# Early row maxima of an attention stage, placed in the Fourier stage by running counts of engine time instead of a fixed list of positions

## The chip, the core and the metric

The kernel runs on one NeuronCore of a Trainium2 chip. The engines of that core work side by side: the matmul engine (PE, with PEld for its weight loads), the vector engine (DVE), the activation engine (ACT), the general engine (POOL) and the engine that issues most transfers (SP). Each takes its own instructions in program order, and they wait for each other through semaphores. The metric is the device time of one execution in microseconds; lower is better. Three executions of the kernel before took 3697.72, 3699.8 and 3702.65 us, so its median is 3699.8 us.

## What is computed

Two identical layers run one after the other on a sequence of 2048 rows of 512 values. Each layer is a Fourier stage and an attention stage, both on a layer-normed input and both added to the input:

```python
def _A_ref(x, dft_seq_re, dft_seq_im, dft_hid_re, dft_hid_im):
    a = jnp.einsum("bsd,ed->bse", x, dft_hid_re)
    b = jnp.einsum("bsd,ed->bse", x, dft_hid_im)
    return jnp.einsum("ts,bse->bte", dft_seq_re, a) - jnp.einsum("ts,bse->bte", dft_seq_im, b)

def _B_ref(x, wq, wk, wv, wo):        # 32 query heads of 16 values, one key head, one value head
    ...
    scores = jnp.einsum("bhqd,bkd->bhqk", q, k) * (Dh ** -0.5)
    p = _softmax(scores, axis=-1)
    o = jnp.einsum("bhqk,bkd->bhqd", p, v)
    return o.transpose(0, 2, 1, 3).reshape(B, S, H * Dh) @ wo

x = x + _A_ref(_layernorm(x), ...)    # Fourier stage, layer 0
x = x + _B_ref(_layernorm(x), ...)    # attention stage, layer 0
x = x + _A_ref(_layernorm(x), ...)    # layer 1, the same two again
x = x + _B_ref(_layernorm(x), ...)
```

The softmax needs the largest score of every row of every head: 32 heads times 2048 rows, each over 2048 keys.

## The kernel before, in words

**Precision.** Values are split into a high and a low part, and a product is three matmuls (high by high, high by low, low by high; `mm3`, lines 85 to 88).

**Fourier stage** (`phase_a`, line 562). The output rows are made in four blocks (`tb`) of 512 rows. A block has 32 steps `n` in which the transforming matrix is multiplied with the normed input (the result is called z, held in the four PSUM banks named x), 16 for the real part (c=0) and 16 for the imaginary part (c=1). Then come the z-by-hidden-matrix products of that block (`y_rows`, line 415, also in the x banks). From step 16 on, a product with 128 rows of the array is written as two products with 64 rows that run beside each other (`z_rows`, line 676); after each first phase ACT copies a few values to `junk` (line 693), which orders the two halves. At the end of c=0 and of c=1, `evac` (line 665) moves z from the x banks to SBUF with ACT, DVE and POOL.

**Work that rides along.** While block tb+1 is in its first steps, the tasks of `prep_tasks` (line 526) normalise block tb, transpose it (`tr_tile`, bank z), make its keys and values (`kv`, line 279, bank y), transpose the values (`v_tr`, bank z), make its queries (`q_mm`, four of them, bank y) and store those to a DRAM buffer `qd` (`q_store`, SP). The tasks are keyed by step: `do_kv` at the sixth step after the block's start, the four `q_mm` at steps 7 to 10, each store one step later.

**Early maxima.** The attention stage needs, for each of 16 query tiles i and four key blocks kb, 16 pairs of heads: `max_pair` (line 353) issues two 64-row matmuls of queries by keys into two banks named y and two DVE reductions that read them (line 359). There are three y banks and one z bank. Part of this work is done in the Fourier stage as soon as queries and keys are there: the list `EARLY` (lines 35 to 40) holds 16 entries (i, kb, slot, load step, first position, last position). A position counts 40 to a block: 32 steps and 8 positions for `y_rows`. `phase_a` (lines 598 to 605) spreads the 16 pairs of an entry evenly over its interval and hooks each behind one group of six matmuls. `qT_load` (line 374) fetches a query tile of 1 MB from `qd` by SP at the load step. Results of tiles other than 0 go to a tile `mxe` and are copied by POOL when the tile's own array is made (`partial`, line 345). Early entries of the two layers are the same.

**Attention stage** (`phase_b`, line 942). For each of 512 steps it issues four score matmuls, two exponentials on ACT (line 803), four products with the values two steps behind (line 814), and the maxima that are left (`max_half`, line 368; the list `units`, line 765, has 1520 of them, each a single matmul and a single reduction, lines 371 and 372). `owed` (line 775) paces them at three per step plus a few after each output projection.

The planner of the kernel is the Python itself: the order in which instructions are written down is the order in which each engine takes them.

## Time and profile before

| quantity | value |
|---|---|
| median of three executions | 3699.8 us |
| profiled execution, its own time | 3704.5 us |
| span of the profiled execution | 3702.7 us |
| PE busy | 3611.1 us, 98% |
| DVE busy | 2803.8 us, 76% |
| ACT busy | 2390.8 us, 65% |
| POOL busy | 775.7 us, 21% |
| mean granted PE clock | 0.992 |

The Fourier stage of layer 0 runs from the start to about 687 us, its attention stage to about 1850 us, the Fourier stage of layer 1 to about 2527 us, and its attention stage to the end. A group row of the profile reads: line, engine, operation, output and inputs, shapes, count, then busy time in us, mean ns of one, then the idle time of the engine just before these instructions and what ended it. A wait row says which engine and line waited for which, in us in total, how often, and the longest one. A window row gives a stretch, its length, the busy time of each engine with the instruction count, the granted PE clock and the share of the DMA engines. In the chain of waits each row is start, length, and the instruction or transfer on which the end of the execution hung. The ends of matmuls are modelled, so a busy PE is not a PE that streams all the time.

### The profile page before, as it was taken

How to read it: one execution, taken by the hardware profiler on the slowest of the kernel's cores; microseconds unless marked ns; L12 is line 12 of the kernel's file. 1: busy time of each engine (PE TensorE's matmuls, PEld its weight loads, DVE VectorE, ACT ScalarE, POOL GpSimd, SP SyncE). 2: the span in 40 equal slices, each digit the busy share in tenths (PEclk: the TensorE clock that was granted, in tenths of full speed). 3: DMA queues.
4: the chain of work that ended last, by engine and by line, in shares of the span. 5: the costliest groups of instructions: out<-in, count | busy, mean ns of one | idle time of the engine just before them, and what ended most of it. 6: DMA issues, size and time to landing. Idle time of an engine off the chain costs nothing. (4 is left out here: it accounts for less than half of the span.)

```text
span 3702.7 us, 64514 instructions
## 1 busy us (share of the span) xinstructions
PE 3611.1 (98%) x25474; PEld 1905.9 (51%) x25474; DVE 2803.8 (76%) x4819; ACT 2390.8 (65%) x3068; POOL 775.7 (21%) x984
## 2 busy tenths in 40 slices
PE   8999999999999999999999999999999999999999
PEld 6776768533433343334387766684343334333433
DVE  5157978788888888888411779778888888888882
ACT  3322222688888888888933231217888888888888
POOL 5544332111111111111254342421000000000000
PEclk9999999999999999999999999999999999999999
DMA  5444241311111101110143342313111111001100
GB/s 176 127 145 124 98 115 58 101 33 50 33 34 33 50 22 25 33 47 24 39 132 104 131 125 92 109 60 96 48 33 36 33 48 35 22 22 50 33 23 26
DMA packets 204736, 243.00 MB, mean 66 GB/s; under 512 B 36880, under 2 KB 160784, under 8 KB 197264
## 3 DMA queue, kind: packets, MB, share of 16 engines
q1 hardware_dynamic: 199504, 222.08, 20.3%
q0 software_dynamic: 4864, 16.78, 1.6%
q8 instruction: 199, 3.26, 0.4%
q14 instruction: 105, 0.86, 0.1%
q10 hardware_dynamic: 64, 0.02, 0.0%
HBM read 174.58 MB, written 63.17 MB: 64 GB/s over the span
## 5 line engine op out<-in xcount | busy, mean ns | idle before, releaser
L803 ACT ACTIVATE slot<-x 128x1024 f32<-128x1024 f32 x1990 | 1942.0, 1027 | 323.9 <-PE x L800 253.2
L372 DVE TENSOR_REDUCE mxp<-y 128x1 f32<-128x512 f32 x3040 | 1910.4, 684 | 254.3 <-PE y L371 204.9
L814 PE MATMUL z<-slot,v 128*32 128x512 f32 x8192 | 1096.4, 605 | 1.5 <-ACT row L817 1.5
L800 PE MATMUL x<-slot,kz 64*128 64x512 f32 x2956 | 890.6, 447 | 2.6 <-DMA slot<-mt 1.1
L800 PEld LDWEIGHTS x<-slot,kz 64*128 64x128 f32 x2956 | 368.0, 185 | 736.6 <-ACT slot L803 600.5
L371 PE MATMUL y<-kz,slot 64*128 64x512 f32 x2208 | 713.2, 432 | 1.4 <-DVE mxp L372 0.6
L359 DVE TENSOR_REDUCE mxe<-y 128x1 f32<-128x512 f32 x832 | 516.2, 682 | 186.0 <-PE y L357 179.2
L687 PE MATMUL x<-ch,xnh 64*128 64x512 f32 (+1 forms) x2048 | 510.7, 389 | 17.0 <-DVE slot L74 9.2
L687 PE MATMUL x<-ch,xnl 64*128 64x512 f32 (+1 forms) x2048 | 478.4, 368 | 0.0
L687 PE MATMUL x<-cl,xnh 64*128 64x512 f32 (+1 forms) x2048 | 477.8, 367 | 0.0
L371 PEld LDWEIGHTS y<-kz,slot 64*128 64x128 f32 x2208 | 347.6, 185 | 79.1 <-DVE mxp L372 20.4
L357 PE MATMUL y<-kz,slot 64*128 64x512 f32 (+1 forms) x1088 | 353.1, 418 | 35.4 <-DVE mxe L359 22.7
L854 POOL TENSOR_TENSOR row<-row,row 128x256 f32<-128x256 f32 x63 | 46.2, 733 | 1581.9 <-DMA row<-rd 1197.1
L78 POOL TENSOR_TENSOR cl<-craw,ch 128x512 fp32r<-128x512 f32 x236 | 302.6, 1300 | 290.2 <-ACT ch L77 223.8
L687 PEld LDWEIGHTS x<-ch,xnh 64*128 64x128 f32 x2048 | 271.5, 188 | 68.8 <-issue 16.2
L814 PEld LDWEIGHTS z<-slot,v 128*32 128x32 f32 x8192 | 163.7, 108 | 275.0 <-issue 248.0
L687 PEld LDWEIGHTS x<-ch,xnl 64*128 64x128 f32 x2048 | 284.2, 188 | 32.5
L687 PEld LDWEIGHTS x<-cl,xnh 64*128 64x128 f32 x2048 | 284.8, 189 | 26.5
L77 ACT CAST ch<-craw 128x512 fp32r<-128x512 f32 x256 | 154.8, 620 | 164.5 <-PE x L687 92.9
L693 ACT COPY junk<-x 128x2 f32<-128x2 f32 x256 | 40.5, 158 | 330.5 <-PE x L687 257.6
L357 PEld LDWEIGHTS y<-kz,slot 64*128 64x128 f32 x1088 | 170.7, 187 | 132.0 <-DVE mxe L359 92.6
L359 DVE TENSOR_REDUCE mxp<-y 128x1 f32<-128x512 f32 (+1 forms) x256 | 144.4, 617 | 24.6 <-PE y L357 21.4
(151 smaller groups left out, 3131.0 us busy)
## 6 DMA issues: line engine op xcount, KB each, us to landing
craw<-ct_in SPq DMA_DIRECT2D x112, 512.0 KB
slot<-qd SPq DMA_DIRECT2D x44, 1024.0 KB
qd<-row SPq DMA_DIRECT2D x144, 128.0 KB
od<-row SPq DMA_DIRECT2D x252, 64.0 KB
row<-x_in SPq DMA_DIRECT2D x32, 256.0 KB
mid<-row POOLq DMA_DIRECT2D x32, 256.0 KB, 2.4
craw<-ct_in SPq DMA_DIRECT2D x32, 256.0 KB
row<-mid SPq DMA_DIRECT2D x32, 256.0 KB
```

The lines of the kernel that those rows point to most:

```text
L77: nc.scalar.copy(hi, raw)
L78: (eng or nc.vector).tensor_sub(lo, raw, f(hi))
L357: nc.tensor.matmul(pm[g], o.qT[i][gs, pr, :], kz[gs, c0:c0 + n], start=True, stop=True)
L359: nc.vector.reduce_max(to[:, g:g + 1], pm[g], axis=AX.X)
L371: nc.tensor.matmul(pm, o.qT[i][gs, pr, :], kz[gs, kb * 512:kb * 512 + 512], start=True, stop=True)
L372: nc.vector.reduce_max(partial(i)[:, pr, g, kb:kb + 1], pm, axis=AX.X)
L687: nc.tensor.matmul(z[d][:, cols], w, hl[j][t == 1][rs_], start=m == 0 and ph == 0 and j == t == 0, stop=j == 1 and t == 2 and (ph == 0 or ...
L693: nc.scalar.copy(junk, zp[dd][:, :, cols.start])
L800: nc.tensor.matmul(st["e"][:, g, :], kz[64 * g:64 * g + KR, c * P:(c + 1) * P], o.qT[i][64 * g:64 * g + KR, cp:cp + 4, :], start=True, sto ...
L803: nc.scalar.activation(ptiles[i, s_][:, 2 * w:2 * w + 2, :], st.pop("e"), AF.Exp, scale=DH ** -0.5)
L814: nc.tensor.matmul(a[32 * j:32 * j + 32, :], v1[:, c, :], pt[:, j, :], start=c == 0, stop=c == NT - 1)
L854: nc.gpsimd.tensor_mul(bt["ot"][:, cs], bt["ot"][:, cs], bt["den"][:, cs])
```

## The change

`EARLY` keeps its 16 pairs of tile and key block, but its last two numbers are now the first and last position at which the entry may be taken, and these windows overlap. A class `Pace` keeps a running time for PE, DVE, ACT and POOL while the instructions are written, and the time at which the three y banks and the z bank come free. After every two matmuls of `z_rows` and of `y_rows` the function `feed` looks for the first entry whose window is open and issues one pair if its two banks are counted as free within 0.3 us of PE's count; behind the ninth step of a block it may use the z bank for the first of the pair. What is not placed by position 149 is left to the attention stage: `taken` records it, `units` is filled at the end of the Fourier stage, and `owed` allows one more per twelve steps, up to 32. Keys, values, queries and stores move one step sooner, and the first two query weights are split at step 4 instead of 5. Steps 16 to 31 of the first block are no longer written as 64-row halves. Results of tiles 1 to 3 go to the tile's own array. Entry (4, 1) uses the same loaded tile as (4, 0).

```diff
 EARLY = [
-    (2, 0, 2, 44, 55, 63), (3, 0, 3, 45, 63, 71), (0, 0, 8, 47, 71, 79.5), (1, 0, 9, 50, 79.5, 88),
-    (2, 1, 0, 65, 88, 92), (0, 1, 8, None, 92, 98), (1, 1, 9, None, 98, 104.5), (4, 0, 2, 79, 104.5, 110.5),
-    (6, 0, 8, 82, 110.5, 116.5), (6, 1, 8, None, 116.5, 122), (7, 0, 9, 88, 122, 126), (4, 1, 0, 96, 126, 130),
-    (7, 1, 9, None, 130, 135), (5, 0, 2, 107, 135.5, 140.5), (0, 2, 8, 99, 140.5, 145), (7, 2, 9, None, 145, 149),
+    (2, 0, 2, 43, 54.5, 70), (3, 0, 3, 46, 58, 70), (0, 0, 8, 48, 60, 89), (1, 0, 9, 52, 63, 91),
+    (2, 1, 0, 65, 86.25, 93.5), (0, 1, 8, None, 86.25, 101), (4, 0, 2, 78, 95, 109.5), (4, 1, 2, None, 95, 109.5),
+    (1, 1, 9, None, 86.25, 119.5), (6, 0, 8, 86, 106, 149), (6, 1, 8, None, 106, 130), (7, 0, 9, 96, 123.5, 149),
+    (7, 1, 9, None, 123.5, 149), (5, 0, 2, 106, 134.5, 143), (0, 2, 8, 104, 130, 149), (7, 2, 9, None, 130, 149),
 ]
-KEPT = [e for e in EARLY if e[0]]
+KEPT = [e[:2] for e in EARLY if e[0] > 3]
...
+    class Pace:
+        pe = dve = act = pool = at = 0.0
+        y = [0.0, 0.0, 0.0]
+        z = 0.0
+        rows = 128
...
+    def shape_to(rows):
+        if rows != Pace.rows:
+            Pace.rows = rows
+            Pace.pe += 0.16
+
+    def mm(out_, w, x, **k):
+        shape_to(x.shape[0])
+        Pace.pe += free(x) / 512 * (0.117 if x.shape[0] <= 64 else 0.233)
+        nc.tensor.matmul(out_, w, x, **k)
...
+                if self.name == "dve":
+                    Pace.dve = max(Pace.dve, Pace.pe + 0.4) + 0.07 + n / 960
+                elif self.name == "act":
+                    Pace.act = max(Pace.act, Pace.pe + 0.3) + 0.1 + n / 1000
...
     def bank(tag):
+        if tag == "y":
+            Pace.y = Pace.y[1:] + [Pace.pe + 4.0]
+        else:
+            Pace.z = Pace.pe + 2.0
         return ps.tile([P, 512], F32, name=tag, bufs={"y": 3, "z": 1}[tag])
...
-        def max_pair(i, pr, c0, n, to):
-            pm = [bank("y")[:, :n], bank("y")[:, :n]]
+        def max_pair(i, pr, c0, n, to, tags="yy"):
+            pm = [bank(tag)[:, :n] for tag in tags]
...
+        def read(tags, g, at):
+            if tags[g] == "z":
+                Pace.z = at
+            else:
+                Pace.y[g - 2 if tags == "yy" else -1] = at
+
+        taken = {e[:2]: NPAIR for e in EARLY}
+        ahead = {e: list(range(NPAIR)) for e in range(len(EARLY))}
+
+        def feed():
+            e = next((e for e in ahead if EARLY[e][4] <= Pace.at < EARLY[e][5]), None)
+            if e is None:
+                return
+            n = Pace.at % 40
+            tags = "zy" if n > 9 and Pace.z < Pace.y[1] else "yy"
+            if max(Pace.z if tags == "zy" else Pace.y[1], Pace.y[0]) > Pace.pe + 0.3:
+                return
+            pr = ahead[e].pop(0)
             i, kb = EARLY[e][:2]
...
+            to = partial(i)[:, pr, :, kb] if i < 4 else st["mxe"][:, KEPT.index((i, kb)), pr]
+            max_pair(i, pr, kb * 512, 512, to, tags)
+            if not ahead[e]:
+                del ahead[e]
...
-            ts[5] = [lambda: wq_split(0), lambda: wq_split(1)]
-            ts[6] = [do_kv]
-            ts[7] = [lambda: v_tr(4 * tb, 4, st["vt"])]
-            ts[8] = []
+            ts[4] += [lambda: wq_split(0), lambda: wq_split(1)]
+            ts[5] = [do_kv]
+            ts[6] = [lambda: v_tr(4 * tb, 4, st["vt"])]
+            ts[7] = []
             for g in range(4):
-                ts[7 + g].append(lambda g=g: q_mm(tb, g, *st["xt"]))
+                ts[6 + g].append(lambda g=g: q_mm(tb, g, *st["xt"]))
                 if g < 2:
-                    ts[7 + g].append(lambda g=g: wq_split(g + 2))
-                ts[8 + g] = [lambda g=g: q_store(tb, g)]
+                    ts[6 + g].append(lambda g=g: wq_split(g + 2))
+                ts[7 + g] = [lambda g=g: q_store(tb, g)]
...
             def by_rows(n):
-                return n >= 16
+                return n >= 32
...
+            def within(n, k, t):
+                Pace.at = 40 * (n // 32) + n % 32 + k / (8 if n >= 112 else 4)
+                if n < 125:
+                    feed()
...
+            for e, left in ahead.items():
+                assert EARLY[e][0]
+                taken[EARLY[e][:2]] = NPAIR - len(left)
+            units.extend((0, pr, g, 3) for pr in range(HALF, NPAIR) for g in range(2))
+            units.extend((i, pr, g, kb) for i in range(1, NT) for pr in range(NPAIR) for kb in range(4) for g in range(2)
+                         if pr >= taken.get((i, kb), 0))
...
         def owed(n):
-            return min(3 * (n + 1) + 12 + o.extra, len(units)) - o.done
+            return min(3 * (n + 1) + 12 + min(n // 12, 32) + o.extra, len(units)) - o.done
```

The remaining lines of the diff send the other instructions of the Fourier stage through wrappers that add to the counts and issue the same instruction as before, and drop a branch of the layer norm that no caller uses.

More of the change, by code (lines that the diff above doesn't have):

```diff
@@ L146, in ln_inv, with ln_rstd @@
         r = rs[:, t0:t0 + n]
-        nc.vector.reciprocal(r, w)
-        nc.gpsimd.tensor_mul(w, r, r)
-        nc.gpsimd.tensor_mul(w, w, v)
-        nc.gpsimd.tensor_scalar(w, w, -0.5, 1.5, op0=ALU.mult, op1=ALU.add)
-        nc.gpsimd.tensor_mul(r, r, w)
-    def ln_rstd(t0, n, table=True, between=lambda: None):
+        vec.reciprocal(r, w)
+        pool.tensor_mul(w, r, r)
+        pool.tensor_mul(w, w, v)
+        pool.tensor_scalar(w, w, -0.5, 1.5, op0=ALU.mult, op1=ALU.add)
+        pool.tensor_mul(r, r, w)
+    def ln_rstd(t0, n):
         v = sb.tile([P, 4], F32, name="lnv", bufs=2)[:, :n]
@@ L347, in partial @@
                 o.mxp[i] = sb.tile([P, NPAIR, 2, 4 if i else 5], F32, name=f"mxp{i % 4}")
-                for e, (i_, kb, *_) in enumerate(KEPT):
+                for e, (i_, kb) in enumerate(KEPT):
                     if i == i_:
-                        nc.gpsimd.tensor_copy(o.mxp[i][:, :, :, kb], st["mxe"][:, e])
+                        np_ = taken[i, kb]
+                        if np_:
+                            pool.tensor_copy(o.mxp[i][:, :np_, :, kb], st["mxe"][:, e, :np_])
             return o.mxp[i]
-        def max_pair(i, pr, c0, n, to):
-            pm = [bank("y")[:, :n], bank("y")[:, :n]]
+        def max_pair(i, pr, c0, n, to, tags="yy"):
+            pm = [bank(tag)[:, :n] for tag in tags]
             for g in range(2):
                 gs = slice(64 * g, 64 * g + KR)
-                nc.tensor.matmul(pm[g], o.qT[i][gs, pr, :], kz[gs, c0:c0 + n], start=True, stop=True)
+                mm(pm[g], o.qT[i][gs, pr, :], kz[gs, c0:c0 + n], start=True, stop=True)
             for g in range(2):
-                nc.vector.reduce_max(to[:, g:g + 1], pm[g], axis=AX.X)
-        def max_early(e, pr):
+                vec.reduce_max(to[:, g:g + 1], pm[g], axis=AX.X)
+                read(tags, g, Pace.dve)
+        def read(tags, g, at):
+            if tags[g] == "z":
+                Pace.z = at
+            else:
+                Pace.y[g - 2 if tags == "yy" else -1] = at
[10 more added lines that the diff above has]
+            pr = ahead[e].pop(0)
             i, kb = EARLY[e][:2]
@@ L505, in ln_split @@
             x = st["xs"][t]
-            nc.scalar.copy(xnh[:, t, :], x)
-            nc.gpsimd.tensor_sub(xnl[:, t, :], x, f(xnh[:, t, :]))
+            act.copy(xnh[:, t, :], x)
+            pool.tensor_sub(xnl[:, t, :], x, f(xnh[:, t, :]))
         def ln_step(n):
@@ L692, in z_rows @@
                         if ph == 0:
-                            nc.scalar.copy(junk, zp[dd][:, :, cols.start])
+                            act.copy(junk, zp[dd][:, :, cols.start])
                         elif m == 7:
@@ L729, in phase_a @@
                             evac(c, (d - 1, d), slice(0, 512))
-                        within((n, d))
                 for fn in tasks.pop(n, ()):
@@ L762, in phase_a @@
                     max_rows(0, 0, HALF, nc.scalar)
-        early = {e[:2] for e in EARLY}
-        units = [(0, pr, g, 3) for pr in range(HALF, NPAIR) for g in range(2)]
-        units += [(i, pr, g, kb) for i in range(1, NT) for pr in range(NPAIR) for kb in range(4) for g in range(2)
-                  if (i, kb) not in early]
+        units = []
         o.done = o.extra = 0
```

197 lines of the change are left out of this document (98 added, 99 removed).

## The prediction

> **What bounds the kernel now.** I read the page first, then the stretches of the two Fourier stages, then the waits, the chain and the timeline inside them.
>
> ```profile
> span 3702.7 us, 64514 instructions
> PE 3611.1 (98%) x25474; PEld 1905.9 (51%) x25474; DVE 2803.8 (76%) x4819; ACT 2390.8 (65%) x3068; POOL 775.7 (21%) x984
> ...
> 204.60:640.00 435.40, 417.19 (x3323) 313.15 (x3325) 349.41 (x586) 108.25 (x264) 154.12 (x130) 0.99 0.34 105
> 2041.80:2479.00 437.20, 418.37 (x3314) 315.27 (x3314) 348.75 (x583) 108.15 (x264) 153.13 (x129) 0.98 0.34 103
> 2160.00:2479.00 319.00, 304.76 (x2394) 224.71 (x2390) 258.61 (x433) 75.67 (x189) 104.95 (x89) 0.98 0.33 98
> 2527.00:3702.70 1175.70, 1164.06 (x7867) 461.21 (x7866) 975.23 (x1629) 1007.10 (x1090) 64.75 (x108) 1.00 0.13 37
> ```
>
> PE sets the length, at 98%. The third and fourth rows are the stretches of layers 0 and 1 from the first early maximum to the end of position 149; their columns are length, PE, PEld, DVE, ACT, POOL, clock. They are alike, so I work on layer 1 and double. PE's busy time hides idle time, since matmul ends are modelled; I therefore count work. The chain shows the unit price where nothing waits:
>
> ```profile
> 2051.37 1.39 PE x L687 x12
> 2052.76 0.23 PE y L357 x2
> ...
> 2171.17 0.23 PE y L87
> ```
>
> Twelve 64-row matmuls take 1.39 us, 0.116 each; a pair of maxima 0.23; one 128-row matmul 0.23. The groups of the stretch 2160 to 2479:
>
> ```profile
> L687 PE MATMUL x<-ch,xnh 64*128 64x512 f32 (+1 forms) x538 | 151.3, 381 | 1.9 <-DVE slot L74 1.7 <-DVE row L437 0.2
> L357 PE MATMUL y<-kz,slot 64*128 64x512 f32 x386 | 142.5, 431 | 11.1 <-DVE mxe L359 9.0 <-DVE kz L290 1.2 <-DVE mxp L359 0.8
> L687 PE MATMUL x<-ch,xnl 64*128 64x512 f32 (+1 forms) x540 | 139.3, 353 | 0.0
> L687 PE MATMUL x<-cl,xnh 64*128 64x512 f32 (+1 forms) x538 | 138.6, 352 | 0.0
> L428 PE MATMUL x<-slot,slot 64*128 64x512 f32 x192 | 30.6, 405 | 0.0
> L86 PE MATMUL y<-slot,slot 128*128 128x512 f32 x48 | 19.8, 412 | 0.6
> L357 PEld LDWEIGHTS y<-kz,slot 64*128 64x128 f32 x386 | 68.5, 188 | 53.8 <-DVE mxe L359 42.7 <-DVE mxp L359 5.4 <-issue 1.6
> L359 DVE TENSOR_REDUCE mxe<-y 128x1 f32<-128x512 f32 x322 | 198.0, 681 | 40.0 <-PE y L357 36.9 <-PE x L687 2.6 <-PE x L428 0.4
> L359 DVE TENSOR_REDUCE mxp<-y 128x1 f32<-128x512 f32 x64 | 39.4, 681 | 1.8 <-PE y L357 1.7
> ```
>
> Of 1616 matmuls of line 687, the 13 steps from 112 on have 48 each of half width: 624 x 0.058 + 992 x 0.116 = 151 us. Maxima and line 428: 578 x 0.116 = 67. Lines 86 to 88, 48 each, and some 12 for the keys: 156 x 0.23 = 36. Transposes and small products: about 4, an estimate. Together 258 of 319 us: **61 us are lost** in this stretch alone. The weight-load row names the main cause: 48.1 us in which a maximum's matmul waits for the reduction that still reads its bank. Yet DVE was idle 40.0 us before those same reductions: maxima come in bursts, then not at all while 128-row work runs. Long waits cost twice:
>
> ```profile
> 2311.93 0.49 PE L357 MATMUL y<-kz,slot 64*128 64x512 f32 x1 [1.40 <-DVE mxe L359]
> ...
> 2299.00:2302.40 3.40, 3.29 (x16) 2.63 (x18) 3.00 (x6) 0.00 (x0) 0.00 (x0) 0.51 0.06 24
> 2312.00:2316.00 4.00, 4.00 (x19) 2.65 (x21) 2.58 (x5) 1.29 (x3) 0.00 (x0) 0.57 0.08 18
> 2400.00:2405.00 5.00, 4.66 (x42) 4.44 (x44) 3.54 (x6) 1.26 (x4) 2.98 (x3) 0.66 0.00 0
> 2465.00:2470.00 5.00, 4.12 (x35) 4.06 (x35) 4.39 (x8) 0.16 (x1) 0.00 (x0) 0.66 0.31 105
> ```
>
> After such waits the granted clock is about half for 3.4 us, which costs some 1.7 us. Four such places lie in the stretch, 7 us.
>
> [...]
>
> **How many pairs are placed.** The diff's counters are sums of constants, so placement can be worked out on paper. Their reduction costs 0.07 + 512/960 = 0.603 us; the trace's burst agrees at 0.604:
>
> ```profile
> 2332.51 8.46 DVE mxe L359 x14
> ```
>
> A step holds 24 half-pairs of z, 2.81 us. With DVE saturated a pair comes every 1.21 us, of which 0.234 is its own matmuls: 2.81/(1.21 - 0.234) = 2.9 pairs a step, 5.5 steps an entry. The four entries that need only the first keys are through about position 77 (54.5 + 4 x 5.5); then nothing is open until 86.25. From there to 149 are 62.75 steps, 11.4 entries; twelve are left, and DVE's other work takes a bit more than a third of an entry, mostly beside the queries' and keys' products. Following the counters through the order, I get 241 pairs of 256 in each layer; 15 pairs of the last entry go to the attention stage.
>
> **The change part by part**, per layer unless said. First, the waits on banks. In 2160 to 2479 their cost lies between 10 us (PE's own idle, 9.0 + 0.8) and 48; 61 lost must be made up of something, and less 7 of clock and some 16 of other gaps (turns between 64 and 128 rows, z's evacuation, keys) 38 remain; I take 38. The new rule issues a pair only when its banks are counted free within 0.3 us, and PE's lateness, which the count leaves out, only gives DVE time; I leave a quarter of the waits. That gives -28. Half the clock places go: -3.5 in layer 1, -2 in layer 0, whose stage shows a clock of 0.99 instead of 0.98. Sixteen pairs fewer in the stretch (one was early, 15 leave): -3.5. Can DVE carry it? 386 reductions took 237.4, 0.615 each; other DVE work is 258.6 - 237.4 = 21. Afterwards 354 x 0.615 + 21 = 239 us in about 284, 84%; today it is 81%. If DVE stays at 81% the stretch becomes 295, a gain of 24 instead of 35: the weak end.
>
> Second, before 2160 the stage has little:
>
> ```profile
> PEld y L357 <- DVE mxe L359: 47.0, 103, 2.8
> PEld y L357 <- DVE mxp L359: 5.4, 18, 1.1
> PEld x L687 <- DVE slot L74: 4.4, 5, 1.1
> ```
>
> 52.4 in the stage less 48.1 leaves 4; I take -3. So the stage gives -38 in layer 1 and -36.5 in layer 0: -74.5.
>
> Third, what is queued behind DVE's maxima. z's evacuation (line 74), the adds of line 437 and the keys (line 290) stand in DVE's order, and PE waits for each before it may reuse a bank. Four banks allow two pairs ahead, 2.5 us, instead of one and a half. Between 0 and 11 places x 1.23 = 13; I take +4, +8 for both, since the x banks are needed a half group later and DVE has often caught up.
>
> Fourth, 30 maxima more in the attention stage.
>
> ```profile
> 3001.37 0.99 PE z L814 x8
> 3003.49 0.99 PE z L814 x8
> 3640.05 1.04 PE z L814 x8
> 3641.94 1.04 PE z L814 x8
> 3002.86 1.89 DVE L372 TENSOR_REDUCE mxp<-y 128x1 f32<-128x512 f32 x3 [0.23 <-PE y L371]
> ```
>
> A step with three maxima takes 2.12 us (3003.49 - 3001.37), one without 1.90: 0.07 us a maximum. The trace has no step with four; there DVE needs 4 x 0.63 = 2.5 us, and the upper end is a whole 0.63 each. Since PE hung on its own work in these steps and DVE has 0.23 to spare in each, I take 0.15: 30 x 0.15 = 4.5 per layer, +9 (4 to 38). `owed` spreads them at one per 12 steps, so they end where the old list ended.
>
> Fifth, steps 16 to 31 of the first block. 384 half matmuls at 0.116 become 192 whole ones at 0.23, the same; 16 `junk` copies fall away. That counts once, in layer 0:
>
> ```profile
> L78 POOL TENSOR_TENSOR cl<-craw,ch 128x512 fp32r<-128x512 f32 x236 | 302.6, 1300 | 290.2 <-ACT ch L77 223.8 <-PE x L687 20.2 <-issue 16.4
> 79.81 0.62 ACT L77 CAST wkvh<-row 128x512 fp32r<-128x512 f32 x1 [4.39 <-DMA row<-wkv_in]
> 81.06 0.79 PE L687 MATMUL x<-ch,xnh 64*128 64x512 f32 x2 [3.12 <-ACT junk L693]
> ```
>
> ACT waits 4.39 us for a weight transfer, and PE waits 3.12 behind the `junk` copy queued there. Without the copy PE waits only if the split of a step two ahead comes late, and that one stands behind the same transfer: between 0 and -6.5 (3.12 and its half clock), I take -3.
>
> Sixth, the keys one step sooner. What moves: two weight splits (two ACT copies, two POOL subtractions), keys, values, four query products, and 24 stores on SP, with the loads behind them. The fourth transposed tile now has half a double step, 24 x 0.116 = 2.8 us, to pass two ACT copies of 0.62 and a POOL subtraction of 1.3 (line 78's row) before the keys need it; ACT copies of the weights wait for a 256 KB load issued 5.6 us earlier instead of 8.4. ACT holds `junk` copies behind it, so a late load would stop PE. Bounds: -1 to +3 per layer; I take +1, +2 in all. The first load of queries:
>
> ```profile
> 2035.14 6.60 DMA slot<-qd
> 2041.79 0.50 PE L357 MATMUL y<-kz,slot 64*128 64x512 f32 x2 [3.02 <-DMA slot<-qd]
> ```
>
> It waits in SP behind the stores, which come a step (2.8 us) sooner, while the first pair asks for it 0.67 step (1.9 us) sooner: the wait shrinks by 0.9, -2 for both layers. Later loads have steps to spare, and (4, 1) saves one of 1 MB. The POOL copies of five entries per layer that fall away lie beside other work: nothing.
>
> Sum: -74.5 + 8 + 9 - 3 + 2 - 2 = -60.5. Against the profiled execution's own 3704.5 us that is 3644; the median is 4.7 us lower, which gives 3639. I say **3640 us** for a median.
>
> **The rivals.** *The waits change their place.* If each of the 11 waits of z's evacuation, adds and keys finds two pairs ahead of it, 11 x 1.23 = 13.5 us and five half-clock spells of 1.7 per layer come back: 22 instead of 4, 36 for both, 3676. For it: line 687's row already names lines 74 and 437 as what ended its idle time. Against it: the longest wait for line 74 is 1.1 us, less than one pair.
>
> *No change.* The same, and DVE-bound steps in the attention stage: 30 x 0.63 = 19 instead of 4.5, 28 more: 3704. Against it is the spare DVE time per step.
>
> *Slower: the clock.* With banks used in turn up to the limit, PE may stop for about a pair, 1.2 us, again and again, and each stop costs 1.7 us of half clock, 2.9 in all. The 70 us that my sum leaves before its +8 are gone at 12 such stops per layer; at 16 (each evacuation, add, key and query product) it is 2 x 16 x 2.9 = 93, and 3640 - 8 + 93 = 3725. For it: the 1.40 us wait was followed by a half clock. Against: the 103 waits average 0.46 us, and the stage's clock stayed at 0.98. [...]
>
> *Better.* All waits go and the half clock with them: (52 + 7 + 3.5) x 2 = 125 instead of 74.5 off, 3590.
>
> *It does not do what it says.* If the counts ran ahead of the chip, pairs would still wait as now; that is the first rival's time or worse, and I give it no share of its own.
>
> **How the numbers follow.** Chances: forecast 0.58 (own range 3612 to 3668: weak end, a gain of 24 in the stretch, +22, and half a dozen for keys and loads; strong end, a tenth of the waits left, -12, the cheap price in the attention stage and the whole `junk` wait, -8, and no term for the third part, -8); better 0.04; changed place 0.20; no change 0.09; slower 0.09. A measurement of this kernel can tell about 0.2%, 7 us, from no change. Faster 0.58 + 0.04 + 0.20 = 0.82, within 0.2% 0.09, slower 0.09. The range of 8 in 10 runs from 3606 to 3690.
>
> **What would show it.** Right: weight loads of the early maxima wait under 20 us per stage for the reductions, the stretch to the last early pair is near 400 us instead of 437, DVE busy there about 84%, 3100 single maxima instead of 3040 in the attention stages, which are 5 us longer each; no `junk` wait near 80 us. Wrong: waits of that size at lines of the evacuation, the adds and the keys; more places at half clock than five in a stage; attention steps with four maxima 0.6 us longer than the others; or a first load that comes later, not sooner.

## The result and the profile after

| | median, us | range of the executions, us |
|---|---|---|
| before (4 executions) | 3700.07 | 3697.72 to 3702.65 |
| after (4 executions) | 3656.82 | 3652.18 to 3658.71 |

The ratio is 0.9881, with a 95% interval of 0.9864 to 0.9898: some 43 us faster. The forecast was 3640 us, with 3612 to 3668 as its own range. The profiled execution of the changed kernel took 3658.71 us, 45.8 less than that of before.

Span, busy time and instructions on the page of the changed kernel:

```profile
span 3656.9 us, 63688 instructions
PE 3569.4 (98%) x25090; PEld 1898.2 (52%) x25090; DVE 2800.2 (77%) x4819; ACT 2387.9 (65%) x3036; POOL 777.8 (21%) x974
```

PE executes 384 matmuls less (192 in each layer's first block, whose halves are written whole) and DVE exactly as many instructions as before: no maximum has gone, some were only moved. The windows of the four stages, first the kernel before (Fourier and attention of layer 0, then of layer 1), then the changed one. The columns are stretch, length, PE, PEld, DVE, ACT and POOL busy, granted clock, share of the DMA engines and GB/s:

```profile
9.10:687.50 678.40, 644.51 (x4873) 488.16 (x4874) 438.71 (x765) 190.94 (x454) 274.95 (x278) 0.98 0.40 117
687.50:1855.90 1168.40, 1160.28 (x7850) 458.89 (x7850) 984.61 (x1713) 1007.09 (x1090) 168.28 (x349) 1.00 0.13 38
1855.90:2526.80 670.90, 642.03 (x4888) 497.44 (x4887) 399.88 (x696) 183.04 (x431) 264.74 (x241) 0.99 0.36 108
2526.80:3702.70 1175.90, 1164.26 (x7868) 461.41 (x7866) 975.43 (x1629) 1007.10 (x1090) 64.75 (x108) 1.00 0.13 37
```

```profile
10.20:649.20 639.00, 609.77 (x4653) 483.41 (x4653) 417.55 (x734) 187.57 (x437) 275.74 (x276) 0.99 0.41 121
649.20:1833.80 1184.60, 1174.85 (x7881) 464.28 (x7879) 1003.77 (x1744) 1008.66 (x1090) 168.29 (x346) 1.00 0.13 38
1833.80:2464.70 630.90, 606.97 (x4664) 483.82 (x4664) 379.72 (x666) 180.19 (x415) 266.25 (x239) 0.99 0.37 113
2464.70:3656.90 1192.20, 1177.83 (x7898) 466.73 (x7896) 993.95 (x1659) 1008.71 (x1090) 64.45 (x105) 1.00 0.13 37
```

The whole reading of the result is in these eight rows. The Fourier stages lose 39.4 and 40.0 us, the attention stages gain 16.2 and 16.3, the start moves by 1.1: -79.4 + 32.5 + 1.1 = -45.8. Of the 32.5 us that the attention stages take back, 9 had been foreseen. (Layer 0's Fourier stage scatters: two runs below that change only the attention stage take 636.8 and 633.3 us for the same instructions, where layer 1's takes 629.8 and 630.3.)

**Fourier stage.** The window from the first early pair to the last one, in the changed kernel, and the rows of the groups in it that count the early maxima:

```profile
2015.60:2415.20 399.60, 384.38 (x3287) 308.51 (x3288) 326.50 (x552) 106.40 (x261) 154.16 (x130) 0.99 0.37 113
```

```profile
L77 PE MATMUL y<-kz,slot 64*128 64x512 f32 x377 | 104.8, 400 | 2.8 <-DVE kz L101 2.6 <-DVE mxe L101 0.2
L77 PE MATMUL z<-kz,slot 64*128 64x512 f32 x105 | 41.4, 394 | 0.7 <-DVE xnl L101 0.4 <-DMA slot<-qd 0.3
```

377 + 105 = 482 matmuls are 241 pairs, the number that the working on paper gave. The stretch is 399.6 us instead of 437.2, and DVE is busy for 326.5 of it, 82% instead of 80%. In the changed kernel every matmul of this part has line 77 and every wrapped operation line 101, since wrappers record them; the tiles tell the groups apart. The weight loads' waits in layer 1's Fourier stage, before (the rows not yet shown), then after:

```profile
PEld x L687 <- DVE slot L74: 7.4, 7, 1.6
...
PEld x L687 <- ACT junk L693: 3.8, 8, 1.1
PEld y L357 <- DMA slot<-qd: 3.4, 1, 3.4
PEld y L86 <- DVE mxe L359: 3.3, 8, 0.4
PEld y L371 <- DVE mxp L372: 3.1, 8, 0.5
PEld x L687 <- DVE row L437: 2.3, 3, 1.0
...
PEld y L357 <- DVE kz L290: 1.1, 2, 0.8
```

```profile
PEld x L77 <- DVE slot L101: 11.1, 8, 1.6
PEld x L77 <- ACT junk L101: 8.2, 12, 1.4
...
PEld y L77 <- DVE mxp L101: 5.8, 20, 0.5
PEld x L77 <- DVE row L101: 5.5, 4, 4.0
...
PEld y L77 <- DVE kz L101: 3.4, 4, 1.8
PEld y L77 <- DVE mxe L101: 2.6, 11, 0.5
```

Waits for a reduction fall from 47.0 + 5.4 + 3.3 + 3.1 = 58.8 us to 5.8 + 2.6 = 8.4, so by 50.4. The wait for the first load of queries is gone from this list. Four others grow: z's evacuation (slot) by 3.7, the copies to `junk` by 4.4, the adds (row) by 3.2, the keys (kz) by 2.3, together 13.6. -50.4 - 3.4 + 13.6 = -40.2, and 15 pairs fewer of 0.234 us are -3.5: this account gives -44 for the stage's -40.0, and three half-clock spells that are gone, some 5 us, are not in it yet (before, the granted clock was 0.50 for about 3.4 us from 2043, 2299, 2312, 2401 and 2466 us, after it only from 2271 and 2353, and one spell lies at the end of the stage in both; 3.4 us at half cost 1.7). So it gives too much. A likely reason, which no run shows by itself, is that a weight load that waits does not always hold a matmul for as long: in the prediction's rows the weight loads of the maxima waited 48.1 us for reductions where PE's own idle time was 9.8.

**Attention stage.** There are 1540 single maxima in the last stage instead of 1510. A step with four of them and the step behind it, in windows of the changed kernel, and then the instructions of the first one from its timeline:

```profile
2995.53:2998.26 2.73, 2.62 (x20) 1.01 (x16) 2.50 (x5) 2.55 (x3) 0.00 (x0) 1.00 1.00 394
2998.26:3000.39 2.13, 2.13 (x21) 0.83 (x17) 1.88 (x4) 1.33 (x3) 0.00 (x0) 1.00 0.22 81
```

```profile
2996.10 2.48 DVE L101 TENSOR_REDUCE mxp<-y 128x1 f32<-128x512 f32 x4 [0.23 <-PE y L77]
...
2996.84 0.18 PEld L77 LDWEIGHTS y<-kz,xnl 64*128 64x128 f32 x1 [0.43 <-DVE mxp L101]
```

The step with four maxima takes 2.73 us, the ordinary one 2.13. The fourth maximum's weights wait 0.43 us for a bank, and DVE's 2.48 us, with the 0.23 that it waits for the first bank, make up the step. A stage has 29 such steps, and three of its 14 steps with seven maxima and an output projection now have eight (6.97 instead of 6.39 us). Over the 30 more maxima the stage's 16.3 us are 0.54 for each; a step that gets one pays 0.6.

### The profile page after: what moved, and what is told of

Its sections match the earlier page's. It is cut to its first block, busy times and chain, and to the rows that moved or that the text cites. A ratio compares the mean times of both kernels' runs of the same rounds, so it can differ in the third digit from the quotient of the medians.

```text
span 3656.9 us, 63688 instructions
## 1 busy us (share of the span) xinstructions
PE 3569.4 (98%) x25090; PEld 1898.2 (52%) x25090; DVE 2800.2 (77%) x4819; ACT 2387.9 (65%) x3036; POOL 777.8 (21%) x974
## 5 line engine op out<-in xcount | busy, mean ns | idle before, releaser
L101 DVE TENSOR_REDUCE mxp<-y 128x1 f32<-128x512 f32 (+1 forms) x3558 | 2219.9, 679 | 277.4 <-PE y L77 236.8
L77 PE MATMUL y<-kz,slot 64*128 64x512 f32 (+1 forms) x3086 | 966.1, 424 | 12.8 <-DVE kz L101 6.1
L77 PE MATMUL x<-ch,xnh 64*128 64x512 f32 (+2 forms) x2048 | 477.7, 378 | 42.1 <-DVE slot L101 15.8
L77 PE MATMUL x<-ch,xnl 64*128 64x512 f32 (+2 forms) x2048 | 470.0, 366 | 1.6 <-POOL xnl L101 1.2
L77 PE MATMUL x<-cl,xnh 64*128 64x512 f32 (+2 forms) x2048 | 466.9, 366 | 0.4 <-POOL cl L101 0.4
L77 PEld LDWEIGHTS x<-ch,xnh 64*128 64x128 f32 (+1 forms) x2048 | 252.2, 187 | 110.3 <-DVE slot L101 22.3
L77 PEld LDWEIGHTS x<-ch,xnl 64*128 64x128 f32 (+1 forms) x2048 | 255.6, 187 | 41.9 <-POOL xnl L101 5.0
L77 PEld LDWEIGHTS x<-cl,xnh 64*128 64x128 f32 (+1 forms) x2048 | 253.3, 188 | 34.9 <-POOL cl L101 0.7
L101 DVE TENSOR_REDUCE mxe<-y 128x1 f32<-128x512 f32 x360 | 226.4, 682 | 28.9 <-PE y L77 28.4
L77 PE MATMUL y<-slot,slot 128*128 128x512 f32 x864 | 221.3, 402 | 6.4 <-DVE mxp L101 5.7
```

Source lines behind the costliest of these rows:

```text
L77: nc.tensor.matmul(out_, w, x, **k)
L101: return fn(out_, in_, *a, **k)
```

## The experiments

The kernel before was run beside each. Runs given with an interval had four executions; the others had a single one, and for them the windows of their traces carry more than the total. The lengths of parts of a stage are taken from the first matmul of a part to the first of the next; a block begins with its first product of z.

### Is the fourth maximum dear because of its place?

The extra maximum is issued before the step's first score instead of behind the second.

```diff
+                four = n % 12 == 0 and owed(n) >= 4
+                if four:
+                    more_max()
                 g = units[o.done][2] if o.done < len(units) else 1
-                for j, m in ((1 - g, 1), (g, 2), (3 - g, 0), (2 + g, 1)):
+                for j, m in ((1 - g, 1), (g, 1 if four else 2), (3 - g, 0), (2 + g, 1)):
```

> The changed kernel with one edit in the attention stage: where a step has four maxima, the additional one is issued first, behind the value products and ahead of the scores, and the step's other three follow one, one and, at the end, one. The count of maxima and their pacing stay. Theory of the bank: the fourth maximum is dear (2.735 us a step against 2.125) because it stands at the end of the step and waits 0.43 us for the oldest of the three y banks; issued first it finds a free bank, and such a step should take 2.25 to 2.4 us, each attention stage 10 to 15 us less, the whole 3627 to 3637 us. Rival, DVE is full: a maximum costs its 0.6 us of DVE wherever it stands; the four-maxima steps or their neighbours keep the time, and the whole stays at 3655 to 3660 us.

Measured: 3653.36 us (3649.17 to 3655.24), ratio 0.9872 (0.9857 to 0.9886). One of its steps with four maxima:

```profile
2487.30:2490.01 2.71, 2.63 (x19) 1.01 (x18) 2.62 (x6) 2.45 (x3) 0.00 (x0) 1.00 0.00 0
```

The median of such steps goes from 2.735 to 2.703 us, no more, and the whole is 3.5 us under the changed kernel, where the theory of the bank had 20 to 30. DVE (the expectations call it VectorE) is busy for 2.62 of 2.71 us: four reductions of 0.62 and some 0.2 us until the first bank is filled are the step, at both places that were tried. The place was not the cause; DVE is the bound of a step with four.

### What is one maximum less worth?

The kernel before, with only the new pacing, so that the same 1520 maxima are taken earlier and the last steps have none.

```diff
-            return min(3 * (n + 1) + 12 + o.extra, len(units)) - o.done
+            return min(3 * (n + 1) + 12 + min(n // 12, 32) + o.extra, len(units)) - o.done
```

> The kernel before with the new pacing alone: one maximum more per twelve steps, up to 32, with the same 1520 maxima in each attention stage, so that the list ends some 11 steps sooner. Theory of the bank: each of the 29 to 32 four-maxima steps costs 0.61 us more, 19 us a stage, less 11 steps at 0.22 us that become steps without maxima; the kernel before gets 14 to 17 us slower per stage, about 3730 us. Rival, DVE is full: the number of reductions is unchanged, so the stage keeps its time, 3700 us.

Measured: 3760.13 us (3754.19 to 3763.95), ratio 1.0156 (1.0139 to 1.0173): 60 us slower, 30 in each attention stage, more than either theory had. A step with four maxima, and the first six steps behind the end of the list, in the last but one tile, which have none:

```profile
2583.12:2585.86 2.74, 2.62 (x18) 1.01 (x17) 2.62 (x6) 2.55 (x3) 0.00 (x0) 1.00 0.00 0
3673.57:3685.84 12.27, 11.70 (x76) 3.27 (x74) 1.39 (x5) 11.73 (x13) 1.90 (x3) 1.00 0.01 3
```

This is the key to the price. Without a maximum these steps take 1.90 to 2.13 us, 2.04 on average, and ACT is busy for 11.73 of the 12.27 us: the two exponentials are their bound. A step with three maxima takes 2.13, so 1.88 us of DVE lie beside the exponentials for 0.08. The fourth makes DVE the longest engine (2.62 us of the 2.74), and the step jumps by a whole reduction, 0.61. An emptied step gives back next to nothing, those 0.08 us for three maxima, so moving a maximum out of a step with three into another one can only cost here.

That is not all of the 30 us. In layer 1's attention stage 38 steps have four maxima (23 us) and four projections have eight (2.4 us). The other large loss, some 8 us, lies in two steps that take 9.26 and 3.89 us: the hurried list had run up to a tile of queries that was not loaded yet, and PE stood for it, in both layers alike. (Together this is a little more than 30; the steps that were emptied gave some of it back.)

```profile
3391.11 0.80 PE L371 MATMUL y<-kz,slot 64*128 64x512 f32 x2 [5.49 <-DMA slot<-qd]
```

The changed kernel has no such wait in its attention stages.

For comparison, the two steps of the kernel before from which the forecast took its price:

```profile
3640.05:3641.94 1.89, 1.89 (x16) 0.67 (x19) 0.00 (x0) 1.89 (x4) 0.82 (x2) 1.00 0.09 27
3001.37:3003.49 2.12, 2.12 (x19) 0.83 (x23) 1.89 (x5) 1.94 (x3) 0.00 (x0) 1.00 0.00 0
```

The first is of the last tile after its list has ended: there two of the four scores go to y banks with exponentials of their own (line 793). It is not the second step without its maxima.

### Can the extra maxima hide in the output projections?

The old pacing, and two more maxima in each output projection (14 of the 15 still find them on the list).

```diff
-            return min(3 * (n + 1) + 12 + min(n // 12, 32) + o.extra, len(units)) - o.done
+            return min(3 * (n + 1) + 12 + o.extra, len(units)) - o.done
...
-                if k % 2 and i < NT - 1:
-                    for _ in range(2):
+                if i < NT - 1:
+                    for _ in range(1 + k % 2):
                         more_max()
                         o.extra += 1
```

> The attention steps keep three maxima; the 30 more of each layer are issued inside the 15 output projections instead, one more behind the first and one more behind the third group of projection products, so a projection holds six extra instead of four. Where the 30 have to wait for VectorE wherever they stand (the theory that VectorE and its three banks are full): a projection step with one maximum more took 6.97 us instead of 6.39, so 30 x 0.58 = 17 us per stage, as now, and 3657 us stays. Rival, that VectorE has idle time in a projection step (four products of a bank each, 6.39 us with 7 reductions of about 0.62 us = 4.3 us) and that the eighth only stood badly behind another: a step of 9 maxima takes 6.4 to 6.6 us, the attention stages lose 13 to 16 us each and the time is 3625 to 3632 us.

Measured: 3654.32 us (3651.44 to 3657.34), ratio 0.9876 (0.9861 to 0.989). The 30 still cost the same; a projection step takes 7.67 us instead of 6.39, 0.64 for each of its two. Not for the reason that the first theory gave, though. From the timeline of such a step:

```profile
2559.72 0.18 PEld L77 LDWEIGHTS y<-kz,xnh 64*128 64x128 f32 x1 [0.36 <-DVE mxp L101]
...
2560.15 0.53 PEld L77 LDWEIGHTS y<-slot,slot 128*128 128x128 f32 x3 [0.25 <-issue]
...
2560.26 0.69 DVE L101 TENSOR_REDUCE mxp<-y 128x1 f32<-128x512 f32 x1 [0.35 <-PE y L77]
```

DVE is not full here: it was idle for 0.35 us before this reduction. But the single 64-row maximum stands between groups of 128-row products, and its weight load waits 0.36 us, the next one of the projection 0.25. In the changed kernel's own projection two maxima follow six products together, and their loads wait as long with no bank behind it:

```profile
2567.42 0.19 PEld L77 LDWEIGHTS y<-kz,xnh 64*128 64x128 f32 x2 [0.37 <-issue]
```

What fits both rows is a turn between the two shapes, 0.6 us there and back, paid once for each place at which maxima are put in, whether one or two. That a maximum here costs the turn and not the bank is read from these waits and not shown by a run of its own; none tried a third maximum at an existing place.

### Which part brings the Fourier stage's gain: the fourth bank or the count?

The kernel before with its fixed list, every second pair of the later steps taking the z bank for one of its two:

```diff
-            max_pair(i, pr, kb * 512, 512, to)
+            n1, n2 = EARLY[e][4:]
+            at = (n1 + pr * (n2 - n1) / NPAIR) % 40
+            max_pair(i, pr, kb * 512, 512, to, "zy" if at > 9 and pr % 2 else "yy")
```

> The kernel before with its fixed positions, but every second early pair behind position 9 of a block takes the z bank for its first half, so that four banks serve. Theory: placement, not the number of banks, is what counts; in bursts DVE needs 1.24 us a pair while pairs come every 0.93, so a fourth bank only delays the wait; waits of maxima fall by less than half and each Fourier stage gains 2 to 15 us. Rival, four banks do it: the waits fall by more than three quarters and each Fourier stage gains 25 us or more, the whole about 3645 us.

And the changed kernel without the z bank; 19 pairs are left instead of 15, and the pacing allows one more maximum per ten steps:

```diff
-            tags = "zy" if n > 9 and Pace.z < Pace.y[1] else "yy"
+            tags = "yy"
...
-            return min(3 * (n + 1) + 12 + min(n // 12, 32) + o.extra, len(units)) - o.done
+            return min(3 * (n + 1) + 12 + min(n // 10, 44) + o.extra, len(units)) - o.done
```

> The changed kernel with the three y banks alone for early maxima (the z bank is never used); by the count 19 pairs are left over instead of 15, so pacing in the attention stage is one more per ten steps. Theory of the fill: with three banks a pair is counted free only when both of its banks are, DVE idles between pairs, PE still does not wait; the Fourier stages change by -3 to +4 us each with four pairs fewer, and weight loads of maxima still wait under 5 us a stage. Rival, the fourth bank removed the waits: with three the waits return to 20 us or more a stage.

Measured: 3679.02 us for four banks with the fixed list, and 3669.92 us for three banks with the count (one execution each). Layer 1's Fourier stage in parts, in us:

| part | before | fixed list, four banks | count, three banks | after |
|---|---|---|---|---|
| first block, and queries at the end | 156.5 | 156.5 | 156.4 | 156.2 |
| second block | 150.9 | 150.7 | 152.3 | 152.3 |
| third block | 176.0 | 169.0 | 163.7 | 161.8 |
| fourth block | 187.5 | 182.1 | 159.3 | 160.6 |
| stage | 670.9 | 658.3 | 631.7 | 630.9 |
| early matmuls in blocks 2, 3, 4 | 98, 212, 202 | 98, 212, 202 | 128, 192, 154 | 128, 198, 156 |

The waits of the weight loads for a reduction of early results, of the fixed list with four banks, then of the count with three:

```profile
PEld y L357 <- DVE mxe L359: 25.3, 55, 2.4
```

```profile
PEld y L77 <- DVE mxp L101: 11.1, 45, 0.7
...
PEld y L77 <- DVE mxe L101: 6.2, 31, 0.5
```

A fourth bank alone nearly halves these waits (47.0 to 25.3) and gives 12.6 us, 7.0 in the third block and 5.4 in the fourth. There the list still puts 202 maxima, and that block stays far the longest. The changed kernel without the fourth bank gives 39.2 us: it puts 30 matmuls more into the second block and 48 fewer into the fourth, and the waits for all reductions fall from 58.8 to 17.3 us, between the two expectations. Of the 39.2, some 4 are the matmuls of the 19 pairs that it leaves to the attention stage; the changed kernel's other edits are in it too, but undone one by one below they move layer 1's stage by about 1 us each. So about 35 us are put down to the count. With the count in place the fourth bank's share in layer 1's stage is 0.8 us. In layer 0 the stage without it is even shorter, 634.8 us against 639.0, within what that stage scatters. What the bank does is four pairs more per layer, 8 maxima that the attention stage need not take. (The whole of the run with three banks is 13 us longer than the changed kernel mainly because its faster pacing gives 42 steps of an attention stage a fourth maximum, instead of 29.)

### How far ahead may the count let a pair go?

A pair may be issued when its banks are counted free within 1.2 us instead of 0.3.

```diff
-            if max(Pace.z if tags == "zy" else Pace.y[1], Pace.y[0]) > Pace.pe + 0.3:
+            if max(Pace.z if tags == "zy" else Pace.y[1], Pace.y[0]) > Pace.pe + 1.2:
```

> The changed kernel with one number altered: a pair may be issued when its banks are counted free within 1.2 us instead of 0.3 us. Theory: the count of free banks is what removed the waits; now pairs come up to 0.9 us before their banks are free, the weight loads of the maxima wait for the reductions again, 10 us or more per Fourier stage instead of under 3 us, and the reductions stay where DVE is busy, so that the Fourier stages change by no more than -3 to +10 us each. Rival: spreading the pairs was enough and the fine count does nothing; waits stay under 3 us.

Measured: 3706.77 us, one execution. 253 pairs are placed instead of 241. The waits for reductions in layer 1's Fourier stage:

```profile
PEld y L77 <- DVE mxp L101: 10.2, 26, 0.5
...
PEld y L77 <- DVE mxe L101: 6.4, 17, 0.5
```

Such waits double, from 8.4 to 16.6 us, and the stage takes 647.8 us instead of 630.9, more than the theory allowed: 17 us for 12 pairs, 1.4 each; layer 0's takes 13.7 us more, 1.1 each. In the attention stage a pair costs two times 0.54 to 0.61, 1.1 to 1.2. So the last pairs are no cheaper here than there. (The attention stages of this run are 10 and 8 us longer than those of the changed kernel although they have 24 maxima less. The pacing was left as it was: 33 steps have four, and the list once more ran up to a tile that was not loaded, so that PE waits 6.8 us in layer 0 and 5.6 in layer 1 for the queries.)

### The halves of the first block

```diff
             def by_rows(n):
-                return n >= 32
+                return n >= 16
```

> The changed kernel with steps 16 to 31 of the first block again written as 64-row halves with their junk copies. Theory: the halves cost no PE time by themselves, the junk copy behind the late transfer of the key and value weights does; layer 0's first block gets 4 to 6.5 us longer with a wait for junk near 80 us, layer 1's stays within 0.5 us; the whole 3661 to 3664 us. Rival, whole matmuls are cheaper as such: both layers' first blocks get longer by the same.

Measured: 3659.82 us (3658.2 to 3660.75), ratio 0.989 (0.9875 to 0.9905). From PE's timeline near 80 us:

```profile
81.27 0.80 PE L77 MATMUL x<-ch,xnh 64*128 64x512 f32 x2 [3.25 <-ACT junk L101]
```

The wait of before is back, and with it a half clock: behind it the pairs of matmuls start 0.43 us apart (81.86, 82.29, 82.71), as behind the wait in the kernel before, whose granted clock was 0.52 from 80 to 87 us; ahead of it they started 0.23 apart there. Layer 0's first block takes 104.4 us instead of 98.4, layer 1's stays at 96.0. So the edit is worth 6.0 us in the block. The whole differs by 3 us, less than this measurement tells.

### The keys one step sooner

The keys, values, queries and stores, and the positions of the entries that need the first ones, one step later again.

```diff
-            ts[4] += [lambda: wq_split(0), lambda: wq_split(1)]
-            ts[5] = [do_kv]
-            ts[6] = [lambda: v_tr(4 * tb, 4, st["vt"])]
-            ts[7] = []
+            ts[5] = [lambda: wq_split(0), lambda: wq_split(1)]
+            ts[6] = [do_kv]
+            ts[7] = [lambda: v_tr(4 * tb, 4, st["vt"])]
+            ts[8] = []
```

> The changed kernel with keys, values, queries, weight splits and stores at the steps of the kernel before (first load at 44, first windows at 55.25 and 87.25 so that the data are there). Theory: the early step buys a window that opens one step sooner, and costs new junk waits (two per block, 5 us a stage) because ACT's weight copies now wait for a later transfer; without it those waits fall to under 2 us a stage, three to five pairs more are left over, and the Fourier stages change by -4 to +2 us each. Rival, the early keys carry the gain: the Fourier stages get 8 us or more longer.

Measured: 3659.45 us, one execution. In layer 1's Fourier stage the `junk` wait goes back, and the first query load is late again:

```profile
PEld x L77 <- ACT junk L101: 5.9, 12, 1.1
```

```profile
2017.92 0.47 PE L77 MATMUL z<-kz,slot 64*128 64x512 f32 x1 [2.46 <-DMA slot<-qd]
```

2.3 us of `junk`, less than the theory had, against 2.5 of the load: the stage takes 631.8 instead of 630.9 us, and 240 pairs are placed, one fewer. The edit changes nothing that can be told.

### The waits that grew

First the second half of each full-width evacuation of the real part goes over ACT and POOL (ScalarE and GpSimd in the expectations), as the imaginary part's does already:

```diff
-                    if cols != slice(0, 512) or (k and not c):
+                    if cols != slice(0, 512):
```

> The changed kernel with z of the real part moved out of the banks by ACT and POOL alone in full-width blocks (the kernel before and the changed one do half of it on DVE). Theory: PE's waits at the second half of z stand behind DVE's maxima; without DVE there the z waits for that line fall from 4.4 us a stage (full-width ones) to under 2 us, ACT having time to spare, and the Fourier stages get 2 to 5 us shorter each. Rival: ACT's own three copies in a row take as long; the waits only change their name and the stage stays within 1 us.

Then the same edit together with the one in the projections, and together with the fourth maximum at the head of its step:

> The same, and the second half of each full-width evacuation goes over ScalarE and GpSimd instead of VectorE, as in the single execution of that change alone (3650.1 us against 3656.8). If the two gains are of different stages they add up: 3650 with projections that hide nothing, 3618 to 3626 with projections that do. In the Fourier stage of the second layer the waits of the next rows' first product for an evacuation of VectorE (about 7 us by the trace of the changed kernel) are gone, and the stage takes 628 instead of 631 us.

> The evacuation over ScalarE and GpSimd, with the fourth maximum of a step issued first in the step. The evacuation's theory: -2.5 us in the second layer's Fourier stage and -5 in the first's; the fourth maximum first: -3 us in all, as measured. Together 3646 us; rival, that the 7 us of the single execution were scatter between executions: 3653 us.

Measured: 3650.14 us for the edit alone (one execution), 3653.72 us (3647.24 to 3655.41, ratio 0.9871, 0.9855 to 0.9886) and 3649.82 us (3649.13 to 3651.86, ratio 0.9863, 0.9846 to 0.9879). Against the same kernels without it that is -7, -0.6 and -3.5 us: at most a few, below what can be told, although three pairs more per layer are placed (244). Layer 1's stage takes 628.4, 629.3 and 629.1 us. The waits of the edit alone say why it is not more:

```profile
PEld x L77 <- ACT row L101: 10.1, 12, 1.7
```

The 11.1 us for an evacuation on DVE are gone, but those for an evacuation on ACT (row) go from 2.3 to 10.1. The rival was right about the waits: most of them only changed their name.

The longest single wait was left, that of the fourth block's first product for two adds. In the changed kernel it is at 2271.05:

```profile
2271.05 0.80 PE L77 MATMUL x<-ch,xnh 64*128 64x512 f32 x2 [3.52 <-DVE row L101]
```

PE stands still while DVE works through reductions and statistics that stand ahead of the adds; then the granted clock is 0.50 from 2271.10 to 2274.50, 3.4 us (the windows are shown in the last section). The last run takes no early pair in the last five of the 32 groups of the hidden-matrix products, with the two edits above:

```diff
             def within_y(tb, k):
                 Pace.at = 40 * tb + 32 + k / 4
-                feed()
+                if k < 27:
+                    feed()
```

> The evacuation over ScalarE and GpSimd, the fourth maximum first in its step, and no early pair in the last 5 of the 32 groups of the hidden-matrix products. The theory of a wait that changed its place (the third part): behind the third block's products the next block's first product waits 3.5 us for two adds that stand behind four reductions and two statistics in VectorE's order; with the reductions gone the wait falls to 1.7 us, as in the kernel before, and the pairs find another place in the block that follows, so each Fourier stage loses some 2 us and the whole goes from 3650 to 3646 us. Rival, VectorE as the bound of the whole dense part: what isn't placed there stays over for the attention stage at 2 x 0.57 us a pair, some two or three pairs per layer, and the time is 3650 to 3654 us.

Measured: 3642.09 us (3638.51 to 3644.36), ratio 0.9839 (0.9822 to 0.9856), the fastest kernel of this study. The same place in its timeline, and the row of the waits:

```profile
2257.65 0.50 PE L77 MATMUL x<-ch,xnh 64*128 64x512 f32 x2 [0.44 <-DVE row L101]
```

```profile
PEld x L77 <- DVE row L101: 2.3, 3, 0.9
```

3.52 us of standing became 0.44, without the half clock behind it: the next pairs of matmuls start 0.23 us apart (2257.99, 2258.22, 2258.45) where in the changed kernel they start 0.43 apart (2271.64, 2272.07, 2272.49), and the granted clock of layer 1's stage is 1.00 instead of 0.99. The Fourier stages take some 4 us less each than with the two edits alone (633.0 and 625.0 us), and one pair less per layer is placed. Together that is as much as the measured 7.7 us, though layer 0's part by itself is no larger than that stage's scatter. The theory of a wait that had changed its place is shown for this wait; the rival, that every pair not placed there is lost, is not.

## Why the prediction was right or wrong

The direction and the mechanism were right: reductions that hold a bank, and maxima that come in bursts, were what the Fourier stage lost time by. The forecast was 17 us too low, and the term that was mis-sized is **the fourth part, the price of 30 more maxima in the attention stage.** That the time still fell inside the range of 3612 to 3668 us is in part luck: the Fourier stages gained 9.9 us more than forecast, and without that the time would have been near 3665.

- **First and second, the waits on banks: -74.5 for both layers.** The net of all Fourier terms was -74.5 + 8 - 3 + 2 - 2 = -69.5; measured -79.4. "I leave a quarter of the waits" was too cautious: a seventh is left (8.4 of 58.8 us of weight-load waits), far under the 20 us that was named as the sign. The stretch of 400 us (399.6) and the 241 pairs came out; DVE is busy 82%, not 84%. The forecast credited bank and count together and did not split them; the runs do: nearly all of it is the count.
- **Third, what is queued behind DVE's maxima: +4 per layer.** Mis-sized. In layer 1 the waits for evacuation, adds and keys grow by 3.7 + 3.2 + 2.3 = 9.2 us, within the bounds of 0 to 13 but nearer the upper one; the last run showed 4 of them to be a real loss, one wait of 3.5 us and its half clock, 1.7. The copies to `junk`, which grew by 4.4, stood in the sixth part.
- **Fourth: +9, measured +32.5.** The step of the working that failed is "a step with three maxima takes 2.12 us, one without 1.90: 0.07 us a maximum". The 1.90 came from a step of the last tile whose scores go other ways. The ordinary step takes 2.04 us on average without any maximum, so the first three cost 0.03 each and the fourth 0.61: the price is not one per maximum, but a jump where DVE becomes the longest engine. The row with which this could have been seen was quoted: 4 x 0.63 = 2.5 us of DVE, more than the step's 2.12. It stood as the upper bound (38 us for both layers), and the value chosen, near the wrong end, rested on 0.23 us of spare DVE time, which is the wait for the first bank and comes again in each step.
- **Fifth, steps 16 to 31: -3 in layer 0, measured -6.0** in that block, the upper end, by the run that undid it.
- **Sixth, keys sooner: +2, first load: -2.** Together nothing, and nothing was measured. Their sizes were not right: in layer 1 the load's wait went from 3.0 us to 0.3, in layer 0 it stayed (4.2 before, 4.8 after), and `junk` took back 2.3 in layer 1.
- **The rivals.** *Waits change their place* was half right: 13.6 us per layer did, against the 22 it gave for waits and clock together, while the stage still gained more than forecast. *No change* had the right price of an attention step (0.63 for 0.61 measured in steps) but needed the other rival's losses as well. *Slower: the clock* did not come: layer 1's Fourier stage shows two half-clock spells (0.50 for 3.4 us each) between its first and its last early pair, at 2271 and 2353 us, where before had five, the four of the forecast among them.

The sum by its own steps: -60.5, less 9.9 for the Fourier stages, plus 23.5 for the attention stages, plus 1.1 for the start is -45.8, the difference of the two profiled executions.

## What to carry to other kernels

Before pricing an addition to a repeated step, add up each engine's time in that step and look for the longest: in these steps work on a shorter engine was nearly free up to the longest one's length (1.88 us of DVE for 0.08) and cost its full time from there on (0.61 for the next reduction), and a step of another shape was no measure for it. When buffers are the visible wait, ask first whether the work is spread as its reader can take it; here the spreading gave about 35 us of a stage where the additional buffer alone gave 13, and next to nothing on top. Work that is taken earlier needs its inputs earlier: two lists that ran ahead of their loads paid some 6 to 8 us a stage. After such a change look for the longest single wait that is new: keeping filler work away from the end of one phase was worth another 8 us.

## What the hardware showed that was not expected

- A single 64-row product between 128-row products cost 0.64 us in the projection steps, as much as a maximum in a step where DVE is full (0.61). The weight loads on its two sides wait 0.36 and 0.25 us; a turn between the two shapes fits, but no run isolates it.
- The length of a wait alone does not tell where the half clock comes. In the changed kernel it begins at 199.2, 455.2, 537.1, 646.3, 2271.1, 2353.0 and 2462.2 us; all the differences are whole multiples of 3.413 us (75, 24, 32, 476, 24, 32), a step worked out from these seven times: 2263.0 us from the first to the last are 663 of it. Windows of the changed kernel on this grid, in pairs of one and the next:

```profile
192.35:195.76 3.41, 1.68 (x16) 1.03 (x12) 0.00 (x0) 0.84 (x3) 2.52 (x2) 1.00 0.79 273
195.76:199.18 3.42, 0.34 (x4) 0.36 (x5) 0.00 (x0) 0.00 (x0) 0.00 (x0) 1.00 1.01 368
...
2267.70:2271.10 3.40, 0.05 (x2) 0.05 (x2) 3.40 (x7) 0.09 (x1) 0.41 (x1) 0.99 0.15 57
2271.10:2274.50 3.40, 3.40 (x16) 2.75 (x18) 3.21 (x5) 0.05 (x1) 3.21 (x4) 0.50 0.42 157
...
2349.60:2353.00 3.40, 1.73 (x22) 1.48 (x24) 2.73 (x6) 2.28 (x5) 2.04 (x3) 1.00 0.00 0
2353.00:2356.40 3.40, 3.40 (x34) 3.31 (x34) 1.91 (x4) 0.68 (x2) 2.11 (x2) 0.50 0.00 0
...
2131.15:2134.57 3.42, 2.10 (x15) 1.54 (x17) 2.80 (x5) 1.50 (x4) 2.47 (x2) 1.00 0.00 0
2134.57:2137.98 3.41, 3.41 (x23) 2.58 (x20) 2.35 (x4) 0.21 (x1) 0.08 (x1) 1.00 0.02 5
```

  Grid windows in which PE was busy for 0.05 and 1.73 us were followed by one at half clock (0.50). The one with 2.10 us, which holds most of a wait of 1.38 us for the keys, was not (1.00), and neither was the one at 192.35 with 1.68, behind which the clock stayed at 1.00. So two waits of 1.00 and 1.34 us (until 2349.93 and 2352.49, both for an evacuation on DVE), of which 1.67 us lie in one of these windows, were followed by a spell, and the longer one of 1.38 us beside work was not; with about half a window busy, 1.73 and 1.68 us, it went both ways, and these rows don't say what decides there.
- An evacuation moved from DVE to ACT and POOL, which are busy for 30% and 44% of that stage, took nearly as long until the bank was free: 10.1 us of waits instead of 11.1 + 2.3.
